# Odd-channel differences by GpSimd before the stacking transfers, with new queue orders

## The chip, the cores and the metric

The kernel runs on one core of a Trainium2 chip. The metric is the device time of one execution in microseconds (us). A core has five engines with a queue each: TensorE (PE, with its weight loads shown apart as PEld), VectorE (DVE), ScalarE (ACT), GpSimd (POOL) and SyncE (SP, which here only issues transfers). Each works through its own list in order and waits on semaphores where a value comes from another engine or from a transfer.

## The reference

The computation is a causal convolution with 15 taps and dilation 2 over 2 sequences of 16000 steps and 144 channels, to 288 channels, then a gate and a projection:

```
B, T, D, K = 2, 16000, 144, 15          # all bf16
xp = jnp.pad(x, ((0, 0), (pad, 0), (0, 0)))          # pad = (K-1)*2
h = sum over i of einsum('btc,cd->btd', xp[:, pad-2*i : pad-2*i+T, :], w[i])
f, g = h[..., :D], h[..., D:]
z = tanh(f) * sigmoid(g)
out = z @ w_o
```

## The kernel before

The 32000 time steps are cut into 128 runs of 250, one on each partition. A tile is one step of all runs; eight tiles are an oct, 31 octs follow two odd tiles at the start, and two octs (o0 = 2m+1, o1 = 2m+2) make the pair m. For each pair there are two units u (r = 0 and 1), 30 in all, each giving four tiles of either oct. The convolution is done with fewer products than 15 a tile: sums of weights meet tiles, and single weights meet differences of tiles. Tiles of x must have channels on the partitions, so they are transposed.

**The 144 channels are split.** The first 128 (DA) go through STA (a packed copy of part of Xr, the raw chunk of 16 tiles) and a DMA transpose into XA (`load_xa`). DVE then makes their differences: V, DU, DD (`v_first`, `v_second`, `v_third`) and, over octs, GX, GU, GV, GD (`g_diffs`). The last 16 channels (DB, the "odd" ones) can't fill an array, so eight taps are stacked on the partitions: XB of an oct holds in partitions 16j to 16j+15 the odd channels of the tile that lies 4j tiles back. `compact_chunk` copies them packed into C16; `load_xb(o)` transposes 128 columns of it (T16, a DMA transpose), drains T16 to a DRAM tensor s16, and fills XB's slot: partitions 32 to 127 from partitions 0 to 95 of the oct before (XB<-XB), 0 to 15 and 16 to 31 from s16 (XB<-s). `b_diffs` (DVE, line 887 by way of `tt`) then makes BD, the differences of XB's tiles, in eight tiles per oct.

**One unit on PE.** CV and CD build the terms common to both octs, which ACT copies between banks of PSUM (line 1132) and evicts to UD and UC (lines 629, 632); XC and XR build others (XS and, by DVE at line 1159, UE, which lies in Xp's room); POOL adds UC and XS into UX (`UP`, line 1169). EF adds UE and UX into the banks on DVE (line 1233, PS<-PS,Xp and PS<-PS,UX). DD closes each bank with products of GD by single weights and one product of BD by WB[v]; XR uses XB itself with WB[2] = WB[0] + WB[1]. ACT does sigmoid and tanh (`halves`), DVE multiplies them (`gate`, line 1006) into Z, a DMA transpose gives ZT, and PE projects it (line 1089) into OS, which is stored.

**Start.** The first ten outputs are computed directly with all taps (`direct`, `direct_b`, then `quad`), while weights land; XB for octs -1 and 0 comes from PE transposes evicted by ACT (line 813). DVE makes the sums of weights in that time (line 822). POOL zeroes WOR and Z and issues the 16 loads of w_o (line 1369).

**Order.** Every operation is added to a graph with what it reads and writes; `schedule` orders the five queues by a list scheduler, and `replay` changes that order by a long table of moves (MOVES) and moves some packed copies from DVE to ACT (ON_ACT, `free_copy`). Waits follow from reads, writes and buffers. `lock=True` marks DVE and POOL operations that the order keeps from overlapping. The rings: 2 chunks of Xr and C16, 2 tiles T16, 6 octs of XB, 4 octs of BD.

Of the kernel before, what the change touches and what calls it, by code (L numbers as in the profile page):

```python
# [122 lines left out]
class _Graph:  # L123
# [42 lines left out]
    def schedule(self, passes=10):  # L166

        users = {}
        for op in self.ops:
            for d in op.deps | op.soft:  # L170
                users.setdefault(d, []).append(op)
        best = None
        late, hint = {}, {}
        for _ in range(passes):
            span = self.run(users, late, hint)
            if best is None or span < best[0] - 1e-6:
                best = (span, dict((e, list(o)) for e, o in self.order.items()), [(op.start, op.end, op.bdeps, [b.phys for b in op.banks]) for op in self.ops])
            hint = dict((op, op.start) for op in self.ops)
            late = {}
            seq = {}  # L180
            extra = {}
            for a, b in zip(self.order["pe"], self.order["pe"][1:]):
                seq[a] = b
            for op in self.ops:
                for d in op.bdeps:
                    extra.setdefault(d, []).append(op)
            for op in sorted(self.ops, key=lambda o: -o.start):
# [1359 lines left out]
```

## Time and profile before

| what | value |
|---|---|
| time of one execution, median of 3 | 308.0 us (307.81 to 308.18) |
| span of the profiled execution, first to last instruction | 306.0 us |
| PE busy | 299.4 us (98%), 2553 matmuls |
| DVE busy | 288.7 us (94%) |
| ACT busy | 260.8 us (85%) |
| POOL busy | 100.1 us (33%) |
| hardware transfer queue | 47.62 MB, 67.3% of the 16 DMA engines |

The profiled execution has no time of its own beside its span; the median of the three timed ones is 2.0 us above it. Busy time is the union of an engine's instructions. A matmul is shown longer than the distance between two of them, because they are pipelined, so a busy PE can still hide gaps of a fraction of a microsecond. A wait is put down to the last thing that ended before the engine went on.

### The profile page before, as it was taken

To read this page: it belongs to the slowest core of one execution; us is meant where nothing else is said; L and a number is where in the kernel's file an instruction comes from. 1 tells how busy PE (TensorE), PEld (TensorE's weight loads), DVE (VectorE), ACT (ScalarE), POOL (GpSimd) and SP (SyncE) were. 2 spreads that over 40 slices of the span, in tenths; PEclk is the share of its full clock that TensorE was granted. 3 is DMA by queue.
4 is the path that set the end of the run, shared out by engine and by line. 5 is a ranking of instruction groups with operands and counts; after the bars stand their busy time and mean duration, and the time that the engine had idled before them with its cause. 6 is when DMAs were issued, how large, how long until landed. Compare 5 with 4: busy or idle time off the path is not lost.

```text
span 306.0 us, 7398 instructions
## 1 busy us (share of the span) xinstructions
PE 299.4 (98%) x2553; PEld 235.5 (77%) x2553; DVE 288.7 (94%) x647; ACT 260.8 (85%) x776; POOL 100.1 (33%) x89
## 2 busy tenths in 40 slices
PE   8999899999999999999999999999999999999995
PEld 7867576877877778878777778777877887777784
DVE  1899999999999999999999999999999999999855
ACT  3678588898889988888998898899888889988885
POOL 7570341233333123333222333321333331233330
PEclk9999999999999999999999999999999999999999
DMA  7978656766657675775689697996647763692643
GB/s 211 296 143 148 143 143 136 177 168 131 214 118 195 133 163 172 177 165 120 191 201 119 193 138 207 127 225 141 169 142 175 213 135 77 184 115 19 176 108 127
DMA packets 100385, 48.47 MB, mean 158 GB/s; under 512 B 88286, under 2 KB 91166, under 8 KB 100348
## 3 DMA queue, kind: packets, MB, share of 16 engines
q1 hardware_dynamic: 99801, 47.62, 67.3%
q8 instruction: 20, 0.33, 0.5%
q0 software_dynamic: 512, 0.33, 0.5%
q14 instruction: 18, 0.14, 0.2%
q10 hardware_dynamic: 34, 0.05, 0.1%
HBM read 13.77 MB, written 10.20 MB: 78 GB/s over the span
## 4 chain that ended last, share of the span: by engine, by line
PE 88%; ACT 4%; DVE 2%; DMA 2%; SPq 2%; issue 1%; DVEq 0%; ACTq 0%
PE PS L979 78%; PE PS L1089 9%; ACT STA L847 1%; DMA WA<-in_w_dram 1%; ACT TG L629 1%; DMA XB<-XB 1%; SPq L671 1%; ACT PS L1132 1%; DVE V L887 1%; DVE WC L822 0%; ACT L629 0%; SPq L874 0%; PE PS L1049 0%; ACT XB L813 0%; DVE PS L1233 0%
## 5 line engine op out<-in xcount | busy, mean ns | idle before, releaser
L1169 POOL TENSOR_TENSOR UX<-UC,XS 128x576 f32<-128x576 f32 x60 | 84.0, 1422 | 192.5 <-ACT UC L629 134.7
L979 PE MATMUL PS<-WA,GD 128*128 128x288 bf16 x450 | 87.7, 286 | 0.8 <-DVE PS L1233 0.8
L1132 ACT ACTIVATE PS<-PS 128x288 f32<-128x288 f32 x213 | 80.5, 420 | 4.5 <-PE PS L979 4.1
L629 ACT ACTIVATE TG<-PS 128x288 bf16<-128x288 f32 x194 | 68.4, 416 | 11.9 <-PE PS L979 11.4
L979 PE MATMUL PS<-WB,BD 128*128 128x288 bf16 x240 | 67.5, 286 | 0.0
L1032 ACT ACTIVATE OS<-PS 128x432 bf16<-128x432 f32 (+1 forms) x93 | 43.0, 492 | 15.5 <-PE PS L1089 14.1
L979 PEld LDWEIGHTS PS<-WA,GD 128*128 128x128 bf16 x450 | 41.9, 98 | 14.3 <-DVE PS L1233 2.1
L1233 DVE TENSOR_TENSOR PS<-PS,Xp 128x288 f32<-128x288 f32 x120 | 49.7, 458 | 1.0 <-ACT OS L1032 0.3
L1233 DVE TENSOR_TENSOR PS<-PS,UX 128x288 f32<-128x288 f32 x120 | 49.6, 456 | 0.0
L1159 DVE TENSOR_TENSOR Xp<-PS,UD 128x576 f32<-128x576 f32 x60 | 42.9, 751 | 3.0 <-PE PS L979 2.7
L979 PE MATMUL PS<-WS,GU 128*128 128x288 bf16 x210 | 44.9, 286 | 0.0
L1089 PE MATMUL PS<-WOR,ZT 128*128 128x144 bf16 (+1 forms) x322 | 40.2, 253 | 0.4 <-ACT XS L632 0.4
L979 PE MATMUL PS<-WB,XB 128*128 128x288 bf16 x140 | 38.2, 286 | 0.0
L979 PE MATMUL PS<-WC,GV 128*128 128x288 bf16 x210 | 36.2, 286 | 0.0
L979 PE MATMUL PS<-WD,DD 128*128 128x288 bf16 x210 | 32.5, 286 | 0.1
L1089 PEld LDWEIGHTS PS<-WOR,ZT 128*128 128x128 bf16 x322 | 27.6, 98 | 6.0 <-ACT XS L632 0.7
L1006 DVE TENSOR_TENSOR Z<-TG 128x576 bf16<-128x576 bf16 (+1 forms) x63 | 27.2, 439 | 2.2 <-ACT TG L629 2.2
L979 PEld LDWEIGHTS PS<-WB,BD 128*128 128x128 bf16 x240 | 23.5, 98 | 5.7
L632 ACT ACTIVATE TG<-PS 128x144 bf16<-128x144 f32 x112 | 24.6, 298 | 0.9 <-PE PS L979 0.7
L979 PEld LDWEIGHTS PS<-WD,DD 128*128 128x128 bf16 x210 | 19.6, 98 | 6.6 <-ACT PS L1132 1.2
L979 PE MATMUL PS<-WT,DU 128*128 128x288 bf16 x120 | 24.3, 286 | 0.0
L979 PEld LDWEIGHTS PS<-WS,GU 128*128 128x128 bf16 x210 | 20.3, 98 | 5.2
(94 smaller groups left out, 471.1 us busy)
## 6 DMA issues: line engine op xcount, KB each, us to landing
Xr<-in_x_dram SPq DMA_DIRECT2D x15, 576.0 KB, 4.6
out_dram<-OS SPq DMA_DIRECT2D x30, 288.0 KB, 2.6
XB<-XB SPq DMA_DIRECT2D x30, 192.0 KB, 2.9
XB<-s SPq DMA_DIRECT2D x59, 32.0 KB, 2.5
s<-T SPq DMA_DIRECT2D x30, 32.0 KB, 2.3
WA<-in_w_dram SPq DMA_DIRECT2D x2, 288.0 KB, 4.1
ZT<-Z SPq DMA_TRANSPOSE x32, 3.1
Xp<-in_x_dram SPq DMA_DIRECT2D x2, 252.0 KB, 4.2
```

Source lines behind the costliest of these rows:

```text
L629: return e.activation(bass.AP(t[:].tensor, off + (0 if st > 0 else n), [[row, NP], [st, 2], [1, n]]), bass.AP(PS[:].tensor, lo * 512 + c0, ...
L632: ins = e.activation(bass.AP(t[:].tensor, off + i * n, [[row, NP], [1, n]]), bass.AP(PS[:].tensor, q.phys * 512 + c0, [[8 * 512, NP], [1, ...
L671: return e.dma_start(tile_ap, src)
L847: g.add("act", lambda a, h=h: a.activation(STA[:, q, 4 * h:4 * h + 4, :], Xr[:, ci % NX, i0 + 4 * h:i0 + 4 * h + 4, 0:DA], ACT.Copy), r=[( ...
L979: return lambda t: t.matmul(bank(b), lhsT=lhs(), rhs=rhs(), start=start, stop=True, skip_group_check=True)
L1006: g.add("dve", lambda v: v.tensor_tensor(dst(), TG[:, s, 1, 2 * k:2 * k + n, :], TG[:, s, 0, 2 * k:2 * k + n, :], ALU.mult), r=[("TG", s, ...
L1032: return (lambda e: e.activation(dst(), src(), ACT.Copy)) if eng == "act" else (lambda e: e.tensor_copy(dst(), src()))
L1089: return t.matmul(PS[:, c0:c0 + n * D], lhsT=ZT[:, zt, blk_, :], rhs=WOR[:, wi_:wi_ + n, :].rearrange("p a b -> p (a b)"), start=first, st ...
L1132: g.add("act", lambda e: e.activation(bank(c), bank(b), ACT.Copy), r=[("bank", b)], w=[("bank", c)], dur=0.29, prio=prio)
L1159: return v.tensor_tensor(ue(u % NU, q, 0, 2).rearrange("p (v n) -> p v n", v=2), src, UD[:, u % NUD, :, :], ALU.add)
L1169: op = g.add("pool", lambda p: p.tensor_tensor(UX[:, u % NU, h, :, :], UC[:, 0, :, :], bass.AP(XS[:].tensor, h * N2, [[2 * N2, NP], [0, 2] ...
L1233: g.add("dve", lambda e, dst=dst, src=src, ua=ua: e.tensor_tensor(bank(dst), bank(src), ua(), ALU.add), r=[("bank", src), ("UX", us, h) if ...
```

## The change

Differences of the odd channels are taken before they are stacked, on x as loaded, by POOL. A chunk is loaded with two more tiles ahead of it (18, 648 KB). C16 becomes four groups of six tiles of 16 channels: for each four steps the tiles 0 and 1 themselves (a packed copy on DVE or ACT), and four differences x(t) - x(t-2) (one POOL subtraction per chunk, 128x256). One DMA transpose of three blocks and one drain follow per chunk, where there were two of one block each. XB's slot holds two groups of six tiles (2 x 768 columns) in place of eight tiles (1024 columns), so XB<-XB moves 288 KB and XB<-s 48 KB. `b_diffs` and BD are gone: DD reads its last operand from XB, with WB[0] for v = 0 and WB[3] = -WB[1] (one ACT operation at the start) for v = 1. Oct 0's slot is made by a POOL copy and a DVE subtraction from XBh, a room in UX's second half; oct 2's slot is filled from oct 0 and from s16 in four transfers, not from oct 1.

The scheduler and its moves are gone: TABLE lists the operations of every queue in order, by their numbers, and `place` sets it. ON_ACT has 11 numbers in place of 5. The table is cut below to some stretches that the prediction speaks of.

```diff
-MOVES = {
...
-ON_ACT = (212, 272, 430, 594, 1569,)
+TABLE = {
...
+    "act": ("3 4 5 33 36 51 35 63 53 61 72 43 71 79 81 112 120 110 109 121 170 96 217 142 18 97 174 102 172 107 101 106 214 241 225 243 224 184 245 183 215 261 248 253 250 194 195 263 "
...
+    "pool": ("21 19 24 22 20 75 76 77 204 208 23 113 211 82 218 198 212 201 205 206 197 207 209 199 210 203 200 202 269 270 275 348 361 408 409 430 503 517 590 749 563 564 662 676 722 "
...
+    "sp": ("2 6 7 8 9 10 11 12 13 14 15 16 17 25 26 28 213 114 111 122 118 115 116 124 123 219 117 128 126 119 127 125 258 271 220 216 226 259 304 221 228 223 229 222 426 276 227 273 "
...
+ON_ACT = (112, 217, 429, 589, 748, 1064, 1226, 1385, 1551, 1703, 2029)
...
+    def place(self, table, on_act):
+
         for i in on_act:
             op = self.ops[i]
             op.eng, op.base, op.lock = "act", op.alt, False
+        for e, text in table.items():
+            self.order[e] = [self.ops[int(x)] for x in text.split()]
         span = self.simulate()
...
-    XCH = 16
+    XCH = 18
...
+            g.add("pool", lambda p: p.tensor_copy(XB[:, bslot(0), :, 0:2, :], XBh[:, 4:12, :].rearrange("p (a b) c -> p a b c", a=2)[:, :, 0:2, :]),
+                  r=[("XBh", 0)], w=[("XB", bslot(0), 0)], dur=0.7, lock=True)
+            g.add("dve", lambda v: v.tensor_tensor(XB[:, bslot(0), :, 2:6, :].rearrange("p a b c -> p a (b c)"), XBh[:, 4:12, :].rearrange("p (a b) c -> p a (b c)", a=2),
+                                                   XBh[:, 2:10, :].rearrange("p (a b) c -> p a (b c)", a=2), ALU.subtract),
+                  r=[("XBh", -1), ("XBh", 0)], w=[("XB", bslot(0), 1)], dur=0.6, prio=2, lock=True)
...
+            free_copy(lambda: cc[:, :, 0:2, :], lambda: xr(2, 2), [("Xr", s)], [("C16", s, 0)], 0.13, 0.27)
+            g.add("pool", lambda p: p.tensor_tensor(cc[:, :, 2:6, :], xr(2), xr(0), ALU.subtract), r=[("Xr", s)], w=[("C16", s, 1)], dur=0.6, lock=True)
+            g.add("sp", lambda e: e.dma_start_transpose(T16[:, s, :, :], C16[:, s, :, :].rearrange("p a b -> p (a b)")), r=[("C16", s, 0), ("C16", s, 1)], w=[("T16", s)], dur=1.3, dma="xb", nbytes=3 * 32768)
+            g.add("sp", lambda e: e.dma_start(bass.AP(S16, ci * 384 * 128, [[128, NP], [128 * 128, 3], [1, 128]]), T16[:, s, :, :]), r=[("T16", s)], w=[("S16", ci)], dur=0.5, dma="xb", nbytes=3 * 32768)
...
+            if o != 2:
+                xdma(lambda: flatr(32, 96, s, 0, 2), lambda: flatr(0, 96, bslot(o - 1), 0, 2), xbk(o - 1), [("XB", s, 0)], 96 * GR * 4)
+            else:
+                xdma(lambda: flatr(64, 64, s, 0, 2), lambda: flatr(0, 64, bslot(0), 0, 2), xbk(0), [("XB", s, 0, 0)], 64 * GR * 4)
+                xdma(lambda: flatr(48, DB, s, 0, 1), lambda: flatr(0, DB, bslot(0), 1, 1), xbk(0), [("XB", s, 0, 1)], DB * GR * 2)
+                xdma(lambda: rows(48, DB, s, 1, 1), lambda: s16(0, 1), [("S16", 0)], [("XB", s, 0, 2)], DB * GR * 2)
+                xdma(lambda: rows(32, DB, s, 0, 2), lambda: s16(0, 2), [("S16", 0)], [("XB", s, 0)], DB * GR * 4)
+            xdma(lambda: rows(0, DB, s, 0, 2), lambda: s16(q0, 2), [("S16", ci)], [("XB", s, 2)], DB * GR * 4)
...
-        def b_diffs(o):
-            kb = xbk(o) + xbk(o - 1)
-            ef(XB, NB, bslot, BD, NBD, dslot, "BD", o, kb, True)
...
-                ops.append((lambda v=v: BD[:, dslot(o), v, 2 - 2 * k + r, :], lambda v=v: WB[:, v, :]))
+                ops.append((lambda v=v: XB[:, bslot(o), 1 - k, 4 - 2 * v + r, :], lambda v=v: WB[:, 3 * v, :]))
...
+        g.add("act", lambda a: a.activation(WB[:, 3, :], WB[:, 1, :], ACT.Copy, scale=-1.0), r=[("WB", 1)], w=[("WB", 3)], dur=0.4, prio=2)
...
-        g.schedule(5)
-        _ms = g.replay(MOVES, ON_ACT)
+        g.place(TABLE, ON_ACT)
```

The numbers count the operations in the order in which the kernel adds them: 112, 113, 114 and 115 are chunk 0's packed copy, subtraction, transpose and drain; 217 and 218 chunk 1's copy and subtraction; 430, 590, 749 and so on the subtractions of chunks 3, 4 and 5; 170 the first copy of the quad; 96 and 97 the first sigmoid and tanh; 142 the negated weights; 23 the zeroing of Z; 197 to 212 the loads of w_o; 269 and 270, and further neighbours in POOL's list such as 563 and 564, a unit's two UP additions.

More of the change, by code (lines that the diff above doesn't have):

```diff
@@ L164, in add @@
         return op
[L166 to L187, printed above, removed]
-                t = 1e9 if not (op.eng == "pe" or op in users) else span
-                for u in users.get(op, ()):
-                    if op in u.deps:
-                        t = min(t, late[u] - self.lag(op, u))
-                for u in extra.get(op, ()):
-                    t = min(t, late[u] - self.lag(op, u))
-                if op.eng == "pe":
-                    t = min(t, late[seq[op]] - op.dur) if op in seq else min(t, op.start)
-                late[op] = t
-        self.order = best[1]
-        for op, (a, b, c, d) in zip(self.ops, best[2]):
-            op.start, op.end = a, b
-            for bk, ph in zip(op.banks, d):
-                bk.phys = ph
-        return best[0]
@@ L358, in replay @@
-    def replay(self, moves, on_act):
-        self.simulate()
+    def place(self, table, on_act):
         for i in on_act:
             op = self.ops[i]
-            self.order["dve"].remove(op)
             op.eng, op.base, op.lock = "act", op.alt, False
-            seq = self.order["act"]
-            p = 0
-            while p < len(seq) and seq[p].start < op.start:
-                p += 1
-            seq.insert(p, op)
-        for e, text in moves.items():
-            seq, nums = self.order[e], [int(x) for x in text.split()]
-            for p, q in zip(nums[::2], nums[1::2]):
-                seq.insert(q, seq.pop(p))
+        for e, text in table.items():
+            self.order[e] = [self.ops[int(x)] for x in text.split()]
@@ L574, in _conv_wavenet_kernel @@
         STA = sb("STA", [NP, NST, 8, 128], BF16)
-        C16 = sb("C16", [NP, NX, XCH * DB], BF16)
-        T16 = sb("T16", [NP, 2, 128], BF16)
+        C16 = sb("C16", [NP, NX, 4, 6 * DB], BF16)
+        T16 = sb("T16", [NP, NX, 3, 128], BF16)
         XA = sb("XA", [NP, NA, 8, 128], BF16)
@@ L812, in b_halo @@
                 i0 = oct_of(tiles[0])[1]
-                g.add("act", lambda v, o=o, i0=i0, bb=bb: v.activation(XB[:, bslot(o), i0:8, :].rearrange("p a b -> p (a b)"), PSb[:, bb * 1024 + 128 * i0:bb * 1024 + 1024], ACT.Copy),
-                      r=[("bank", HB[bb])], w=[("XB", bslot(o), i) for i in range(4)], dur=0.5 if o < 0 else 0.95)
+                g.add("act", lambda v, o=o, i0=i0, bb=bb: v.activation(XBh[:, 8 * o + i0 + 4:8 * o + 12, :].rearrange("p a b -> p (a b)"), PSb[:, bb * 1024 + 128 * i0:bb * 1024 + 1024], ACT.Copy),
+                      r=[("bank", HB[bb])], w=[("XBh", o)], dur=0.5 if o < 0 else 0.95)
+            g.add("pool", lambda p: p.tensor_copy(XB[:, bslot(0), :, 0:2, :], XBh[:, 4:12, :].rearrange("p (a b) c -> p a b c", a=2)[:, :, 0:2, :]),
[3 more added lines that the diff above has]
+                  r=[("XBh", -1), ("XBh", 0)], w=[("XB", bslot(0), 1)], dur=0.6, prio=2, lock=True)
         wak = [("WA", i) for i in range(5)]
@@ L830, in load_xchunk, with xr @@
             s = ci % NX
[L831 to L833 removed]
+            return g.add("sp", ld_x(flat(Xr[:, s, 0:c - a + 2, :]), 0, NP, E0 + a - 2, E0 + c), w=[("Xr", s)], dur=0.5, dma="xr", nbytes=NP * (c - a + 2) * D * 2, soft=(chain["sp"],) if ci < 2 else ())
+        NGR = 2 * (NOCT - 1)
+        S16 = nc.dram_tensor("s16", (NGR * 6, DB, 128), BF16).ap().tensor
         def compact_chunk(ci):
[L836 removed]
             s = ci % NX
[L838 to L839 removed]
+            def xr(t, n=4):
+                return bass.AP(Xr[:].tensor, (s * XCH + t) * D + DA, [[NX * XCH * D, NP], [4 * D, 4], [D, n], [1, DB]])
+            cc = C16[:, s, :, :].rearrange("p a (t c) -> p a t c", c=DB)
+            free_copy(lambda: cc[:, :, 0:2, :], lambda: xr(2, 2), [("Xr", s)], [("C16", s, 0)], 0.13, 0.27)
+            g.add("pool", lambda p: p.tensor_tensor(cc[:, :, 2:6, :], xr(2), xr(0), ALU.subtract), r=[("Xr", s)], w=[("C16", s, 1)], dur=0.6, lock=True)
+            g.add("sp", lambda e: e.dma_start_transpose(T16[:, s, :, :], C16[:, s, :, :].rearrange("p a b -> p (a b)")), r=[("C16", s, 0), ("C16", s, 1)], w=[("T16", s)], dur=1.3, dma="xb", nbytes=3 * 32768)
+            g.add("sp", lambda e: e.dma_start(bass.AP(S16, ci * 384 * 128, [[128, NP], [128 * 128, 3], [1, 128]]), T16[:, s, :, :]), r=[("T16", s)], w=[("S16", ci)], dur=0.5, dma="xb", nbytes=3 * 32768)
         def load_xa(o):
@@ L846, in load_xa @@
                 for h in range(2):
-                    g.add("act", lambda a, h=h: a.activation(STA[:, q, 4 * h:4 * h + 4, :], Xr[:, ci % NX, i0 + 4 * h:i0 + 4 * h + 4, 0:DA], ACT.Copy),
+                    g.add("act", lambda a, h=h: a.activation(STA[:, q, 4 * h:4 * h + 4, :], Xr[:, ci % NX, i0 + 2 + 4 * h:i0 + 6 + 4 * h, 0:DA], ACT.Copy),
                           r=[("Xr", ci % NX)], w=[("STA", q, h)], dur=0.5, prio=2)
             else:
-                free_copy(lambda: STA[:, q, :, :], lambda: Xr[:, ci % NX, i0:i0 + 8, 0:DA],
+                free_copy(lambda: STA[:, q, :, :], lambda: Xr[:, ci % NX, i0 + 2:i0 + 10, 0:DA],
                           [("Xr", ci % NX)], [("STA", q, 0), ("STA", q, 1)], 0.34, 1.0)
@@ L855, in xbk @@
         def xbk(o):
-            return [("XB", bslot(o), i) for i in range(4)]
+            return [("XB", bslot(o), i) for i in range(3 if o else 2)] + ([("XB", bslot(o), 1, 0)] if o == 1 else [("XB", bslot(o), 0, i) for i in range(3)] if o == 2 else [])
         def load_xb(o):
-            s, q, ci = bslot(o), o % 2, chunk_of(8 * o)
-            c0 = (8 * o - CH[ci][0]) * DB
-            ROW = NB * 1024
+            s, ci = bslot(o), chunk_of(8 * o)
+            GR = 6 * 128
+            ROW = NB * 2 * GR
@@ L863, in xdma @@
             def xdma(out, in_, r, w, n):
                 g.add("sp", lambda e: e.dma_start(out(), in_()), r=r, w=w, dur=0.5, dma="xb", nbytes=n)
-            def rows(p0, n, slot, i0, i1):
-                return bass.AP(XB[:].tensor, p0 * ROW + slot * 1024 + i0 * 128, [[ROW, n], [128, i1 - i0], [1, 128]])
-            def flatr(p0, n, slot, i0, i1):
-                return bass.AP(XB[:].tensor, p0 * ROW + slot * 1024 + i0 * 128, [[ROW, n], [1, (i1 - i0) * 128]])
-            def s16(t, n):
-                return bass.AP(S16, t * DB * 128, [[128, DB], [DB * 128, n], [1, 128]])
@@ L874, in load_xb, with rows @@
-            g.add("sp", lambda e: e.dma_start_transpose(T16[:, q, :], C16[:, ci % NX, c0:c0 + 128]), r=[("C16", ci % NX)], w=[("T16", q)], dur=1.3, dma="xb", nbytes=32768)
-            xdma(lambda: bass.AP(S16, 8 * o * DB * 128, [[128, NP], [1, 128]]), lambda: T16[:, q, :], [("T16", q)], [("S16", o)], 32768)
-            xdma(lambda: flatr(32, 96, s, 0, 8), lambda: flatr(0, 96, bslot(o - 1), 0, 8), xbk(o - 1), [("XB", s, 0)], 196608)
-            xdma(lambda: rows(0, DB, s, 0, 8), lambda: s16(8 * o, 8), [("S16", o)], [("XB", s, 3)], 32768)
+            def rows(p0, n, slot, g0, ng):
+                return bass.AP(XB[:].tensor, p0 * ROW + (slot * 2 + g0) * GR, [[ROW, n], [128, 6 * ng], [1, 128]])
@@ new lines, in flatr, with s16 @@
+            def flatr(p0, n, slot, g0, ng):
+                return bass.AP(XB[:].tensor, p0 * ROW + (slot * 2 + g0) * GR, [[ROW, n], [1, GR * ng]])
+            def s16(q, n):
+                return bass.AP(S16, q * 6 * DB * 128, [[128, DB], [DB * 128, 6 * n], [1, 128]])
+            q0 = 2 * (o - 1)
+            if o != 2:
[5 more added lines that the diff above has]
+                xdma(lambda: rows(32, DB, s, 0, 2), lambda: s16(0, 2), [("S16", 0)], [("XB", s, 0)], DB * GR * 4)
@@ L878, in load_xb @@
+            xdma(lambda: rows(0, DB, s, 0, 2), lambda: s16(q0, 2), [("S16", ci)], [("XB", s, 2)], DB * GR * 4)
             if o > 1:
-                xdma(lambda: rows(16, DB, s, 0, 8), lambda: s16(8 * o - 4, 8), [("S16", o - 1), ("S16", o)], [("XB", s, 1), ("XB", s, 2)], 32768)
+                xdma(lambda: rows(16, DB, s, 0, 2), lambda: s16(q0 - 1, 2), [("S16", chunk_of(8 * o - 8)), ("S16", ci)], [("XB", s, 1)], DB * GR * 4)
             else:
-                xdma(lambda: flatr(16, DB, s, 0, 4), lambda: flatr(0, DB, bslot(0), 4, 8), xbk(0), [("XB", s, 1)], 16384)
@@ L882, in load_xb @@
-                xdma(lambda: rows(16, DB, s, 4, 8), lambda: s16(8, 4), [("S16", 1)], [("XB", s, 2)], 16384)
+                xdma(lambda: flatr(16, DB, s, 0, 1), lambda: flatr(0, DB, bslot(0), 1, 1), xbk(0), [("XB", s, 1, 0)], DB * GR * 2)
+                xdma(lambda: rows(16, DB, s, 1, 1), lambda: s16(0, 1), [("S16", 0)], [("XB", s, 1)], DB * GR * 2)
         TR = 128
@@ L1239, in DD @@
             p, n = UB[u][h], UB[u][2 + h]
-            we = [("D", vslot(o - i)) for i in range(4)] + [("BD", dslot(o)), ("WB", 0)] + wak
-            wf = [("D", vslot(o - i)) for i in range(4)] + [("BD", dslot(o)), ("WB", 1)] + wak
             k = part
@@ L1280, in direct_b @@
             g.add("pe", region(b, [lambda: xb_tile(e), lambda: xb_tile(e - 2)], [lambda: WB[:, 0, :], lambda: WB[:, 1, :]]),
-                  r=[("XB", bslot(o), i) for o in (-1, 0) for i in range(4)] + [("WB", 0), ("WB", 1)], w=[("bank", b)], dur=2 * MM)
+                  r=[("XBh", -1), ("XBh", 0), ("WB", 0), ("WB", 1)], w=[("bank", b)], dur=2 * MM)
         load_xchunk(0)
```

178 lines of the change are left out of this document (7 added, 171 removed), and 111 rows, old and new, of tables (MOVES, TABLE).

## The prediction

> **What bounds the kernel now.** I read the page's busy shares first, then busy time by stage, then who TensorE (PE) waits for, then the timeline at those waits.
>
> ```profile
> PE 299.4 (98%) x2553; PEld 235.5 (77%) x2553; DVE 288.7 (94%) x647; ACT 260.8 (85%) x776; POOL 100.1 (33%) x89
> ```
> ```profile
> 6.00:28.00 22.00, 21.23 (x189) 16.79 (x190) 19.73 (x56) 16.44 (x36) 10.70 (x20) 1.00 0.89 211
> 28.00:64.00 36.00, 34.55 (x279) 25.01 (x278) 34.71 (x76) 28.68 (x82) 11.67 (x8) 1.00 0.61 141
> 64.00:280.00 216.00, 216.00 (x1832) 171.01 (x1831) 215.07 (x472) 193.18 (x595) 66.80 (x49) 1.00 0.70 159
> ```
>
> The columns are length, then busy time of PE, weight loads, DVE, ACT and POOL, then granted clock and DMA share. From 64 to 280 us PE is busy 216.00 of 216.00 us at clock 1.00, beside a DVE that is busy 215.07. PE sits idle for 0.77 us from 6 to 28 us and for 1.45 us from 28 to 64 us. Waits, longest in total first, say for whom; then the places, with the row before each:
>
> ```profile
> PE PS L746 <- DVE HEAT L677: 1.1, 1, 1.1
> PE PS L979 <- DVE PS L1233: 0.8, 2, 0.6
> PE PS L979 <- ACT PS L1132: 0.7, 1, 0.7
> PE PS L1089 <- ACT XS L632: 0.4, 1, 0.4
> ```
> ```profile
> 17.17 1.39 PE L979 MATMUL PS<-WA,XA 128*128 128x288 bf16 x10
> 19.49 0.54 PE L979 MATMUL PS<-WC,V 128*128 128x288 bf16 x3 [0.68 <-ACT PS L1132]
> 34.85 0.42 PE L1089 MATMUL PS<-WOR,ZT 128*128 128x144 bf16 x3 [0.43 <-ACT XS L632]
> 35.91 0.42 PE L979 MATMUL PS<-WA,GD 128*128 128x288 bf16 x2 [0.65 <-DVE PS L1233]
> 36.91 0.29 PE L979 MATMUL PS<-WB,BD 128*128 128x288 bf16 x1
> 37.26 0.42 PE L979 MATMUL PS<-WT,XA 128*128 128x288 bf16 x2
> 44.65 0.42 PE L979 MATMUL PS<-WA,GD 128*128 128x288 bf16 x2 [0.17 <-DVE PS L1233]
> ```
>
> One matmul shows 0.29 us, yet ten in a row take 1.39: the pitch is (1.39 - 0.29) / 9 = 0.122 us. So each idle time that is shown hides another 0.29 - 0.12 = 0.17 us. The four waits at 19.49, 34.85, 35.91 and 44.65 show 0.68 + 0.43 + 0.65 + 0.17 = 1.93 us and cost 1.93 + 4 x 0.17 = 2.6 us. At 37.26 another 0.35 - 0.12 = 0.23 us goes. That is 2.8 us in places that I can name; I allow some 0.5 for smaller ones, 3.3 us in all. The change keeps all matmuls (the last one of each DD reads XB and WB[3] in place of BD and WB[1]), so nothing can be won from 64 to 280 us; it can only be lost there. The first wait (for HEAT) and the end after the last matmul depend on first loads and last stores, which stay.
>
> **The change part by part.**
>
> *DVE gives up the BD subtractions and part of the C copies.*
>
> ```profile
> L887 DVE TENSOR_TENSOR BD<-XB 128x1024 bf16<-128x1024 bf16 x25 | 16.9, 684 | 0.0
> L887 DVE TENSOR_TENSOR BD<-XB 128x512 bf16<-128x512 bf16 x10 | 4.2, 418 | 0.0
> L887 DVE TENSOR_TENSOR BD<-XB 128x1024 bf16<-128x1024 bf16 (+1 forms) x7 | 4.2, 607 | 0.0
> ```
>
> 16.9 + 4.2 = 21.1 us leave DVE over the run, of which 4.2 us lie before 64 us (third row, the window 0 to 64). One subtraction for oct 0 comes in (0.7 us, as a 128x1024 row). Past 64 us this frees an engine beside which PE does not wait: 0. Before 64 us DVE is busy 34.71 of 36 us and releases two of the four waits, so 3.5 us less in its queue is worth something there.
>
> *The chain that the second oct's odd channels made.* The chain of waits has, ahead of the wait at 35.91:
>
> ```profile
> 30.27 2.61 DMA XB<-XB
> ...
> 33.88 0.60 DVE BD L887
> ```
>
> Oct 2 had to copy oct 1's slot after that had landed. It is now filled from the drained DRAM tensor and from oct 0, without waiting for oct 1, and BD's 0.60 is gone. I count the waits at 34.85, 35.91, 37.26 (0.60 + 0.82 + 0.23 = 1.65 us) as mostly removed: 1.2. It is not all, because the DRAM route is itself late: it starts with chunk 0's GpSimd subtraction (113), which POOL's list now puts behind two WOR issues and the Z memset.
>
> ```profile
> 3.60 2.97 POOL L728 MEMSET Z<- 128x3456 bf16 x1
> 12.36 8.55 POOL L1369 DMA_DIRECT2D WOR<-in_w_o_dram  x16 [0.29 <-DMA WA<-in_w_dram]
> ```
> ```profile
> 16.29 1.22 SPq L874 DMA_TRANSPOSE T<-C  x1
> ```
>
> The WOR issues can't begin before 12.36 (they wait for the last weights); two of them are 2 x 8.55/16 = 1.1 us, the memset 2.97, the subtraction 0.9 (below): it ends near 17.3, so the first transpose goes out 1.0 us after the 16.29 of before. Against that stand the 2.61 + 0.60 us that leave the chain. At 44.65 I count 0.2 of 0.34.
>
> *ACT's new order.* Its list now puts the first copy of the quad (number 170) ahead of the first sigmoid (96) and behind four STA copies and the copy of chunk 0's odd channels (112).
>
> ```profile
> 17.43 1.28 ACT L629 ACT_TABLE_LOAD   x1
> 18.72 0.41 ACT L629 ACTIVATE TG<-PS 128x288 bf16<-128x288 f32 x1
> 19.03 0.41 ACT L1132 ACTIVATE PS<-PS 128x288 f32<-128x288 f32 x1
> 22.79 0.43 ACT L1032 ACTIVATE C<-Xr 128x256 bf16<-128x256 bf16 x1
> ```
>
> The copy that releases PE at 19.49 loses 1.28 + 0.31 us ahead of it and gains about 0.4 of copy 112: some 1.2 us earlier, more than the 0.85 that PE lost. The sigmoid and the tanh end up to 1 us later (copy 112, then chunk 1's copy, the negated WB[3] and a dummy between them), which holds their PSUM banks longer; PE has the quad's other matmuls meanwhile. I take 0.6 of 0.85. Later six more free copies lie on ACT (11 numbers against 5), at 193.18 of 216 us: room for 0.4 to 1.0 us each, hidden.
>
> *POOL's new work: 15 subtractions of 128x256 and one copy of 128x512.* No row has either form. The nearest are:
>
> ```profile
> L1169 POOL TENSOR_TENSOR UX<-UC,XS 128x576 f32<-128x576 f32 x60 | 84.0, 1422 | 192.5 <-ACT UC L629 134.7 <-ACT UC L632 43.8 <-ACT XS L632 14.0
> L804 POOL COPY XS<-Xp 128x32 bf16<-128x32 bf16 x1 | 0.5, 541 | 0.1
> 150.91 2.77 POOL L1169 TENSOR_TENSOR UX<-UC,XS 128x576 f32<-128x576 f32 x2 [6.23 <-ACT UC L629]
> 152.74 0.82 DVE L1233 TENSOR_TENSOR PS<-PS,UX 128x288 f32<-128x288 f32 x2
> ```
>
> Between 0.54 (32 elements) and 1.42 us (576), on the line through both, 256 elements cost 0.54 + 0.88 x 224/544 = 0.90 us. I take 0.9; 15 x 0.9 = 13.5 us on an engine that idles 192.5 us before UX: hidden if it runs in the 6.2 us that POOL waits for UC. The one copy lies between the same two rows, near UX's by its size, 1.3 us; it fills oct 0's slot before the first XB<-XB and lies beside the XA transposes on SP: 0. What can be uncovered is a UX pair behind a subtraction: the first UX ends at 150.91 + 1.41 = 152.32 and DVE reads it at 152.74, 0.42 us later. A subtraction that starts late enough to hold UX by more than that shows on DVE and then on PE.
>
> *The transfers.*
>
> ```profile
> XB<-XB SPq DMA_DIRECT2D x30, 192.0 KB, 2.9
> XB<-s SPq DMA_DIRECT2D x59, 32.0 KB, 2.5
> T<-C SPq DMA_TRANSPOSE x30, 2.6
> XA<-STA SPq DMA_TRANSPOSE x30, 3.3
> Xr<-in_x_dram SPq DMA_DIRECT2D x15, 576.0 KB, 4.6
> ```
>
> XB<-XB grows to 288 KB, XB<-s to 48 KB; T<-C and the drain become 15 of three blocks instead of 30 of one; Xr grows to 648 KB. Landing: XB<-XB between 2.9 and 4.6 (Xr's, twice the bytes), I take 3.2; the transposes between 2.6 and 3.3 (eight blocks), I take 2.8. SP's list has 249 numbers; its issues of before sum to 276, so 15 transposes and 15 drains go and oct 2's extra three come. A lighter queue covers a landing that is 0.3 us longer, with prefetch: the subtractions of chunks 4 and 5 (590 and 749) stand in POOL's list before the UX pair 563 and 564. Cost on the path: 0; if the cover went, 0.3 us an oct, 30 x 0.3 = 9 us.
>
> *Sum.* 1.2 + 0.2 + 0.6 = 2.0 us from the start, 0 past 64 us. The span is 306.0 and the runs' median 308.0, so 2.0 us lie around the span; the same 2.0 off the median gives 306.0.
>
> **The rivals.**
>
> *Stalls move, none goes.* The sigmoid's banks, or the later drained rows of chunk 0, hold PE where ACT and DVE no longer do. For it: the DRAM route has one more step than before (a GpSimd subtraction, and a landing of a transpose and two transfers after it). Against it: BD and the serial copy are really gone. 308.0 +- 0.6.
>
> *Slower: the subtraction ahead of UX.* The trace shows POOL held by DVE once:
>
> ```profile
> 41.92 0.68 DVE L961 TENSOR_TENSOR GU<-DU 128x1024 bf16<-128x1024 bf16 x1
> 42.52 0.45 DVE L1006 TENSOR_TENSOR Z<-TG 128x576 bf16<-128x576 bf16 x1
> 42.05 3.55 POOL L1169 TENSOR_TENSOR UX<-UC,XS 128x576 f32<-128x576 f32 x2 [4.41 <-ACT UC L629]
> ```
>
> The UX pair that began beside DVE's SBUF operations took 3.55 us instead of 2.77, 0.78 longer, which is about until they were through. The new subtraction falls into POOL's waiting time, and that is when DVE does SBUF operations; if it gets through only when DVE turns to PSUM, it stands right ahead of UX, 0.9 - 0.42 = 0.5 us too late, each chunk. Past 64 us lie some 12 of the 15 chunks (216 of about 270 us of units): 6 us, less the 2.0 won: 312. It decides from 0.42 + 2.0/12 = 0.6 us of delay. Against it: DVE has some 1.4 us less to do each chunk (21.1/15), so it can run ahead, and POOL idles over 6 us.
>
> [...]
>
> *More than counted.* All 3.3 us go: 304.7.
>
> **How the numbers follow.** Forecast 0.55 (304.9 to 307.3 by itself: 3.1 to 0.7 us won); more than that 0.05; stalls only move 0.13; the POOL rival 0.20 and longer landings 0.07, both slower. A measurement tells 0.2% (0.6 us) from no change. Faster 0.60, same 0.13, slower 0.27. The range, 304.5 to 310.0, leaves out a little below and the worst of the slower cases, together under 2 in 10.
>
> **What would show it.** Right: PE's waits on DVE PS, ACT PS and ACT XS before 64 us fall from 1.9 us to under 0.8; DVE under 272 us busy; PE full from 64 to 280 us; POOL's subtraction near 0.9 us. Wrong: PE idle past 64 us with DVE PS<-PS,UX behind it (POOL), or DMA XB as releaser (transfers), or new waits on DMA s or XB before 40 us.

## The result and the profile after

The changed kernel takes 313.1 us (median of 5, 311.91 to 314.9) against 308.0: a ratio of 1.0169, interval 1.0144 to 1.0194. It is 1.7% slower, outside the range of the prediction. Medians here are over all executions of a kernel; the ratios leave out the few that lie over 1.5% above the fastest of the same kernel. The profiled execution took 311.91 us, the shortest of the five, with a span of 310.2, against 306.0 before: 4.2 us longer.

The page's busy shares, and busy time by stage (columns as in the prediction):

```profile
PE 299.9 (97%) x2553; PEld 234.1 (75%) x2553; DVE 279.5 (90%) x607; ACT 264.0 (85%) x786; POOL 110.4 (36%) x105
```
```profile
28.00:64.00 36.00, 32.23 (x261) 23.02 (x259) 33.43 (x69) 27.13 (x75) 10.52 (x9) 1.00 0.84 184
64.00:280.00 216.00, 214.53 (x1814) 168.08 (x1813) 203.76 (x436) 195.02 (x606) 72.98 (x59) 1.00 0.82 181
```

PE does the same 2553 matmuls. It is busy 2.32 us less from 28 to 64 us (34.55 before) and 1.47 us less from 64 to 280 us, where it was full: 3.8 of the 4.2 us. The DMA share of these two stages went from 0.61 to 0.84 and from 0.70 to 0.82. PE's waits say for whom, and the timeline where:

```profile
PE PS L811 <- DMA XB<-s: 1.8, 1, 1.8
PE PS L811 <- DVE Xp L991: 1.8, 1, 1.8
PE PS L921 <- DMA ZT<-Z: 1.1, 1, 1.1
```
```profile
24.16 0.42 PE L811 MATMUL PS<-WT,XA 128*128 128x288 bf16 x2 [0.59 <-DVE WT L646]
32.66 0.28 PE L811 MATMUL PS<-WS,GU 128*128 128x288 bf16 x1 [1.83 <-DMA XB<-s]
46.59 0.42 PE L811 MATMUL PS<-WC,GX 128*128 128x288 bf16 x2 [1.83 <-DVE Xp L991]
93.43 0.54 PE L921 MATMUL PS<-WOR,ZT 128*128 128x144 bf16 x4 [1.07 <-DMA ZT<-Z]
```

The waits of before on ACT PS (19.49), ACT XS (34.85) and DVE PS (35.91, 44.65) are gone, but for 0.2 us on DVE PS. In their place stand four others. With the 0.17 us that each hides, they cost 0.8 + 2.0 + 2.0 + 1.2 = 6.0 us, against the 2.8 us named in the prediction: 3.2 of the 4.2 us. The remaining 1.0 us is not traced to a place.

**The wait at 32.66.** GpSimd's timeline (its first row as it was before, then after), then the first transpose in SP's queue, then the landing in the chain of waits:

```profile
10.37 1.09 POOL L797 MEMSET XS<- 1x512 bf16 x2 [3.81 <-ACT XS L740]
```
```profile
11.90 1.09 POOL L615 MEMSET XS<- 1x512 bf16 x2 [8.26 <-ACT XS L558]
13.06 0.60 POOL L622 COPY XS<-Xp 128x32 bf16<-128x32 bf16 x1
13.61 1.24 POOL L1200 DMA_DIRECT2D WOR<-in_w_o_dram  x2
14.85 3.00 POOL L546 MEMSET Z<- 128x3456 bf16 x1
17.79 1.08 POOL L668 TENSOR_TENSOR C<-Xr 128x256 bf16<-128x256 bf16 x1
...
20.72 6.87 POOL L1200 DMA_DIRECT2D WOR<-in_w_o_dram  x13
```
```profile
18.90 1.29 SPq L669 DMA_TRANSPOSE T<-C  x1
...
27.68 3.73 SPq L695 DMA_DIRECT2D XB<-s  x6
```
```profile
29.27 3.30 DMA XB<-s
```

The first transpose goes out at 18.90, 2.6 us later than the 16.29 of before. SP then issues with pauses of 0.1 us at most up to 31.4, so what stands behind it is late too; XB<-s lands at 29.27 + 3.30 = 32.57 and PE starts at 32.66. Before, PE came to these products at 30.77 and did not wait. Thirteen of the 16 loads of w_o now stand behind the zeroing and are issued from 20.72 to 27.6; before, all 16 were out by 20.9. They now run beside XB's transfers; the experiments below come back to this.

**The wait at 46.59.** DVE's timeline, GpSimd's and the chain:

```profile
42.43 1.90 DVE L723 TENSOR_TENSOR DD<-V 128x1024 bf16<-128x1024 bf16 x1
44.25 1.62 DVE L864 COPY STA<-Xr 128x1024 bf16<-128x1024 bf16 x1
45.79 0.74 DVE L991 TENSOR_TENSOR Xp<-PS,UD 128x576 f32<-128x576 f32 x1
```
```profile
42.32 3.26 POOL L1001 TENSOR_TENSOR UX<-UC,XS 128x576 f32<-128x576 f32 x2 [3.99 <-ACT UC L450]
```
```profile
33.79 5.31 DMA XA<-STA
```

XA<-STA took 5.31 us from its issue (median before 3.3) and released DVE late. Then GpSimd began its two UX additions just ahead of DVE's next operation. DD took 1.90 us where it takes 0.68 in the prediction's row of the same shape, and the copy 1.62 where another one, at 40.06, took 0.42: together 2.4 us, most of what PE lost. Each is 1.2 us longer, DD with two inputs and the copy with one, where one UX addition takes 1.41 us (mean of 60) and the first had begun 0.11 us before DD. That the UX pair held DVE, for one addition in each of the two, is an estimate from these lengths and starts.

This wait is not a fixed price of the change. In a second profile of the same kernel (the run for comparison below) GpSimd began 0.03 us after DD, DD ran at its usual length, only the copy was held, and PE waited 0.48 us:

```profile
41.79 3.47 POOL L1001 TENSOR_TENSOR UX<-UC,XS 128x576 f32<-128x576 f32 x2 [4.00 <-ACT UC L450]
```
```profile
41.76 0.69 DVE L723 TENSOR_TENSOR DD<-V 128x1024 bf16<-128x1024 bf16 x1
42.36 1.63 DVE L864 COPY STA<-Xr 128x1024 bf16<-128x1024 bf16 x1
```

In the fourteen profiles of this case the UX pair near this place held two DVE operations in four (PE waited 1.83 to 2.41 us), one in eight (at most 0.48) and none in two (0.17). In the four, GpSimd began before the last but one of DVE's operations ahead of Xp; in the eight, and in the kernel before, after it.

**The wait at 93.43.** SP's queue of that time, and the transfers by kind (size, median us from issue to landing):

```profile
81.58 1.05 SPq L489 DMA_DIRECT2D Xr<-in_x_dram  x1
...
86.61 2.74 SPq L904 DMA_TRANSPOSE ZT<-Z  x1
```
```profile
out_dram<-OS SPq DMA_DIRECT2D x30, 288.0 KB, 3.1
XB<-XB SPq DMA_DIRECT2D x29, 288.0 KB, 3.4
XB<-s SPq DMA_DIRECT2D x60, 48.0 KB, 3.0
ZT<-Z SPq DMA_TRANSPOSE x32, 3.5
XA<-STA SPq DMA_TRANSPOSE x30, 4.2
T<-C SPq DMA_TRANSPOSE x15, 3.2
...
q1 hardware_dynamic: 107049, 53.63, 76.5%
```

The chain has ZT<-Z from 86.61 for 6.78 us, to 93.39, where the median is 3.5; chunk 6's load of 648 KB stands ahead of it in the queue. The queue moves 53.63 MB in place of 47.62, and transfers that did not change became slower: XA<-STA from 3.3 to 4.2 us.

### The profile page after: what moved, and what is told of

Read it like the earlier page. It is cut to its first block, busy times and chain, and to the rows that moved or that the text cites. A ratio compares the mean times of both kernels' runs of the same rounds, so it can differ in the third digit from the quotient of the medians.

```text
span 310.2 us, 7389 instructions
## 1 busy us (share of the span) xinstructions
PE 299.9 (97%) x2553; PEld 234.1 (75%) x2553; DVE 279.5 (90%) x607; ACT 264.0 (85%) x786; POOL 110.4 (36%) x105
## 3 DMA queue, kind: packets, MB, share of 16 engines
q1 hardware_dynamic: 107049, 53.63, 76.5%
## 4 chain that ended last, share of the span: by engine, by line
PE 83%; DMA 8%; DVE 5%; issue 1%; SPq 1%; ACT 1%; DVEq 0%
PE PS L811 72%; PE PS L921 8%; DMA XA<-STA 4%; DMA ZT<-Z 2%; PE PS L564 1%; DMA XB<-s 1%; DVE PS L1065 1%; DVE Xp L991 1%; PE PS L592 1%; DVE V L723 1%; DVE STA L864 1%; DVE DD L723 0%; SPq L695 0%; SPq L669 0%; DVE Z L838 0%
## 5 line engine op out<-in xcount | busy, mean ns | idle before, releaser
L811 PE MATMUL PS<-WB,XB 128*128 128x288 bf16 x360 | 101.8, 286 | 0.0
L964 ACT ACTIVATE PS<-PS 128x288 f32<-128x288 f32 x213 | 81.9, 418 | 7.8 <-PE PS L811 6.4
L450 ACT ACTIVATE TG<-PS 128x288 bf16<-128x288 f32 x180 | 65.1, 418 | 6.8 <-PE PS L811 5.7
L811 PEld LDWEIGHTS PS<-WA,GD 128*128 128x128 bf16 x450 | 40.6, 98 | 15.7 <-DVE PS L1065 2.3
L811 PEld LDWEIGHTS PS<-WB,XB 128*128 128x128 bf16 x360 | 35.2, 98 | 8.7
L811 PE MATMUL PS<-WC,GV 128*128 128x288 bf16 x210 | 37.9, 286 | 0.0
L811 PE MATMUL PS<-WD,DD 128*128 128x288 bf16 x210 | 34.0, 286 | 0.0
L453 ACT ACTIVATE TG<-PS 128x144 bf16<-128x144 f32 x140 | 29.8, 301 | 2.5 <-PE PS L811 1.9
L811 PE MATMUL PS<-WC,GX 128*128 128x288 bf16 x120 | 23.5, 286 | 1.8 <-DVE Xp L991 1.8
L723 DVE TENSOR_TENSOR V<-XA 128x1024 bf16<-128x1024 bf16 (+2 forms) x38 | 23.6, 623 | 1.1 <-DMA XA<-STA 0.9
```

What stands on the lines that cost most here:

```text
L450: return e.activation(bass.AP(t[:].tensor, off + (0 if st > 0 else n), [[row, NP], [st, 2], [1, n]]), bass.AP(PS[:].tensor, lo * 512 + c0, ...
L453: ins = e.activation(bass.AP(t[:].tensor, off + i * n, [[row, NP], [1, n]]), bass.AP(PS[:].tensor, q.phys * 512 + c0, [[8 * 512, NP], [1, ...
L723: return g.add("dve", lambda v: v.tensor_tensor(dst(), a(), b(), ALU.subtract), r=r, w=wk, dur=dur, prio=2, lock=True)
L811: return lambda t: t.matmul(bank(b), lhsT=lhs(), rhs=rhs(), start=start, stop=True, skip_group_check=True)
L964: g.add("act", lambda e: e.activation(bank(c), bank(b), ACT.Copy), r=[("bank", b)], w=[("bank", c)], dur=0.29, prio=prio)
```

## The experiments

Two theories stood first: the start order (chunk 0's subtraction behind the zeroing of Z) and the larger transfers. The rival was GpSimd's new work. Each run's ratio is to the kernel before, measured beside it.

**Chunk 0's subtraction ahead of the zeroing of Z**, all else as changed; the gates wait for the zeroing.

```diff
-"21 19 24 22 20 75 76 77 204 208 23 113 211 82 218
+"21 19 24 22 20 75 76 77 204 208 113 23 211 82 218
```

> The changed kernel with one swap in POOL's list: chunk 0's subtraction goes ahead of the zeroing of Z (the gates now wait for that zeroing by name). Start-order theory: the first T<-C goes out near 16.3 us in place of 18.9, the 2.0 us that PE lost at 32.7 go, and with them part of the 2.0 at 46.6, so 313.1 becomes 309 to 311. Transfer-volume theory: the early gain is given back while the transfer engines are full, 312 to 313.5. POOL theory (subtractions hold UX or DVE all along): within 0.7 of 313.1.

311.19 us, 1.0097 (1.0069 to 1.0125). The first transpose went out at 16.85 and the wait for XB<-s shrank, but that for ZT<-Z grew:

```profile
PE PS L922 <- DMA ZT<-Z: 1.9, 1, 1.9
...
PE PS L811 <- DMA XB<-s: 0.6, 1, 0.6
```

The wait is shorter mainly because PE came 0.96 us later. The transpose was 2.05 us earlier and the XB<-s that PE needs was issued at 27.34 in place of 29.27, but it landed at 32.34 in place of 32.57:

```profile
27.34 5.01 DMA XB<-s
```

PE began these products at 32.39, against 32.66 and, in the second profile of the changed kernel, 32.12. So the place of the subtraction alone does not explain this wait.

**The sizes of before**: a chunk's load without its two extra tiles, and XB's transfers with 8 of 12 blocks from oct 3 on. XB is zeroed once by DVE at the start.

```diff
+            d = 2 if ci > 1 else 0
...
+                xdma(lambda: cut(flatr(32, 96, s, 0, 2), 8 if o > 2 else 12), lambda: cut(flatr(0, 96, bslot(o - 1), 0, 2), 8 if o > 2 else 12), xbk(o - 1), [("XB", s, 0)], 96 * GR * 4)
```

> The changed kernel with its larger transfers cut to the bytes of before: XB<-XB 192 KB and XB<-s 32 KB from oct 3 on, Xr 576 KB from chunk 2 on (so four of the twelve stacked tiles are left as they were, and two tiles of a chunk; the result of those products is not the reference's). XB is zeroed once at the start. Transfer-volume theory: landings return to before's and PE's losses at 46.6 and 93.4 shrink, 309.5 to 311. Start-order theory: the loss at 32.7 comes before any cut transfer, and what follows hangs on it, so 312 to 313.5. POOL theory: no change.

The kernel leaves a third of XB's new columns and two tiles of a chunk as they were. 310.27 us, 1.0084 (1.0054 to 1.0114), with 49.01 MB. The wait for ZT<-Z is gone, its transpose lands in 3.8 us with the smaller load still ahead of it; the early one, which has the same order behind it and the extra zeroing ahead, is longer, and PE's clock over the 5 us from 34 on was 0.66:

```profile
34.98 0.28 PE L817 MATMUL PS<-WS,GU 128*128 128x288 bf16 x1 [3.35 <-DMA XB<-s]
...
36.31 0.69 PE L817 MATMUL PS<-WS,GU 128*128 128x288 bf16 x2
```
```profile
34.00:39.00 5.00, 4.02 (x20) 2.69 (x21) 1.78 (x4) 1.44 (x3) 0.99 (x1) 0.66 0.85 207
```

**The kernel before, with every XB<-XB sent twice**, the second time into a spare slot.

```diff
-            xdma(lambda: flatr(32, 96, s, 0, 8), lambda: flatr(0, 96, bslot(o - 1), 0, 8), xbk(o - 1), [("XB", s, 0)], 196608)
+            xdma(lambda: twice(flatr(32, 96, s, 0, 8), (NB - s) * 1024), lambda: twice(flatr(0, 96, bslot(o - 1), 0, 8), 0), xbk(o - 1), [("XB", s, 0)], 196608)
```

> The kernel before, with each XB<-XB sent twice in one transfer (the second copy into a spare slot), 384 KB in place of 192: 5.8 MB more, about what the change adds (6.0 MB), and no other edit. Transfer-volume theory: 310 to 313, with PE waiting for transfers before 110 us. Start-order and POOL theories: 308.0 to 308.6.

320.2 us, 1.0375 (1.0324 to 1.0426). 53.51 MB, about as many as the changed kernel moves, cost 11 to 12 us in the order of before:

```profile
PE PS L982 <- DVE PS L1236: 3.2, 4, 2.5
PE PS L982 <- DMA XB<-s: 1.7, 1, 1.7
```

So added bytes are not covered in the kernel before either. This one doubles the very transfer that XB waits for, so this is not a price for the same bytes elsewhere.

**GpSimd's subtraction cut to one element from chunk 2 on.**

```diff
+            g.add("pool", lambda p: p.tensor_tensor(cc[:, :, 2:6, :], xr(2), xr(0), ALU.subtract) if ci < 2 else p.memset(C16[:, s, 0, 6 * DB - 1:6 * DB], 0.0), r=[("Xr", s)], w=[("C16", s, 1)], dur=0.6, lock=True)
```

> The changed kernel with POOL's subtractions from chunk 2 on replaced by a memset of one element (0.1 us in place of 0.7; the differences of later chunks stay those of the first two, so the result is not the reference's). POOL theory (my rival: the subtraction ahead of UX, or against DVE's SBUF operations): 1.5 to 5 us faster than 313.1. Start-order and transfer-volume theories: within 0.7 of 313.1.

311.44 us, 1.0110 (1.0057 to 1.0164), with the waits where they were:

```profile
PE PS L811 <- DVE Xp L991: 2.1, 1, 2.1
...
PE PS L811 <- DMA XB<-s: 1.1, 1, 1.1
```

The next run, the changed kernel once more beside other experiments, is the measure for this:

> The changed kernel as it is, on the chip and beside the runs of the others: 312 to 314 by every theory; it is the measure for the rest.

312.08 us, 1.0132 (1.0094 to 1.0170). Against the first measurement of 313.1 the cut run lies 1.7 us lower, in the band that had been set for the GpSimd theory. Against this second one it lies 0.6 us lower, the two intervals overlap widely, and the waits that the theory would remove are still there. So the subtractions past chunk 1 cost nothing that these runs can tell, with a resolution of some 2 us.

The second profile of the changed kernel also shows that its waits move from execution to execution: 1.47 us for XB<-s, 0.48 for Xp, 0.83 for ZT<-Z, and 1.53 at 50.39 for XB<-XB, which the first did not have.

**Order and sizes together** (the first two edits).

> The subtraction of chunk 0 ahead of the zeroing of Z and the larger transfers cut to the bytes of before (part of the stacked tiles left as they were, as in the cut alone). If the early loss is from the start's order and the losses at 46 and 93 us from the bytes, both go: 307.0 to 309.0. If one cause is behind both, no better than the better of the two alone: 310 to 311.5.

309.46 us, 1.0044 (1.0029 to 1.0058). PE no longer waits for ZT<-Z or Xp, but still 2.3 us for XB<-s: the first transpose went out at 16.40, and XB<-s landed at 32.59 all the same.

**The first edit, and in SP's list chunk 6's load (904) behind ZT<-Z (729)**, all bytes kept.

```diff
-438 597 904 584 750 673 592 729 747
+438 597 584 750 673 592 729 904 747
```

> The swap at the start, and the load of chunk 6 (648 KB, issued at 81.6 us in the changed kernel) moved behind the ZT<-Z transpose that was issued at 86.6 and landed at 93.4. Transfer theory (that transpose lands late because the load stands ahead of it in full transfer engines): PE's 2.0 us at 92.6 become under 0.5, and the time falls by 1 to 2 us against the swap alone, to 309.0 to 310.2. If the transpose is late by itself: no change, 311.2 +- 0.6.

309.84 us, 1.0061 (1.0041 to 1.0081). The wait for ZT<-Z is gone here too: this transpose landed 3.2 us after its issue, against 7.0 with the first edit alone. It was late because a load of 648 KB stood ahead of it in the queue.

**Two more moves on top**: the weight sum WT (150) earlier on DVE, and chunk 1's transpose (219) behind the six XB<-s.

```diff
-153 164 160 166 168 150 152
+153 164 160 150 166 168 152
...
-123 219 117 128 126 119 127 125 258
+123 117 128 126 119 127 125 219 258
```

> The same, and two more moves at the start: the weight sum WT ahead of GU and GD on DVE (PE lost 0.8 to 1.1 us for it near 25), and oct 1's and 2's XB<-s ahead of chunk 1's transpose on SP (PE lost 0.8 us for them). Start-order theory: each loss goes, 307.0 to 308.8, about the kernel before. If the transfer engines set the early landings whatever the order: 309 to 310.

311.98 us, 1.0141 (1.0090 to 1.0192): slower, though the profiled execution shows fewer early waits than the one above. The six XB<-s were issued from 24.80 on, 2.9 us sooner than in the changed kernel, and still landed between 29.3 and 32.2, beside the loads of w_o and XB<-XB, so that issuing sooner brought little. Two of the four executions had a mean clock of 0.994 and 0.995 and took 313.1 and 313.8; the other two took 310.6 and 310.9 at 1.000, which is still above most of the run before it. Why stays open.

**The zeroing of Z (23) before GpSimd's two zeroings of XS and the copy behind them (75 to 77)**, so in time in which it idles, on top of the kernel with the late chunk load; then the same with WT earlier (150 as above).

```diff
-"21 19 24 22 20 75 76 77 204 208 113 23 211
+"21 19 24 22 20 23 75 76 77 204 208 113 211
```

> As with the late chunk load, but POOL zeroes Z before its start-up work, in the time in which it idles (3.6 to 11.9 us in the changed kernel), so that chunk 0's subtraction and the loads of w_o come earlier and no zeroing stands beside DVE's work at 18 us. Start-order theory: the waits for WT (1.0 us) and for XB<-s (0.5 us) shrink below half, 308.4 to 309.4 against 309.8. If they hang on the transfer engines alone: 309.8 +- 0.5.

> Z zeroed early and the late chunk load, and on DVE the weight sum WT ahead of GU and GD. If PE's wait for WT near 25 us is a loss by itself: 0.4 to 1.0 us faster than Z early alone. If what PE gains there it waits for the next thing: no difference, +- 0.4.

309.49 us, 1.0033 (1.0001 to 1.0066), and 310.29 us, 1.0069 (1.0039 to 1.0098). The wait for XB<-s is gone in both: PE begins those products at 30.76 and 31.03. SP does not issue the six XB<-s sooner than with the late load alone (from 25.92 on, against 25.49), but the loads of w_o come 3.0 us sooner. GpSimd's loads of w_o, and the landings of XB's transfers issued between about 24 and 33 us, each first with the late load alone, then with Z zeroed early:

```profile
21.32 6.86 POOL L1201 DMA_DIRECT2D WOR<-in_w_o_dram  x13
18.29 6.87 POOL L1201 DMA_DIRECT2D WOR<-in_w_o_dram  x13
```
```profile
DMA to landing us min/median/max: 4.2/5.1/5.4
DMA to landing us min/median/max: 1.8/2.9/3.7
```

So the place of the zeroing decided the wait at 32.66. That it did so by way of the loads of w_o is read from these rows; the loads were not moved alone. In the first of the two kernels one wait of size is left in the start, 2.0 us for Xp, where DVE's DD took 1.89 us and the copy 1.61 beside a UX pair again. Moving WT gained nothing. The second kernel's waits are all 0.7 us or less beside the first one for HEAT; its ten executions fall into five from 308.9 to 309.6, the profiled one among them, and five from 311.0 to 312.4. That in the second group two DVE operations were held is possible, but not shown.

**The kernel before, with the quad's first copy ahead of the first sigmoid on ACT**: the one part of the change that the prediction valued at 0.6 us, alone.

```diff
+        seq = self.order["act"]
+        seq.remove(self.quad_copy)
+        seq.insert(seq.index(self.first_tanh[0]), self.quad_copy)
```

> The kernel before with one move: the quad's first copy goes ahead of the first sigmoid on ACT, as in the changed kernel. My step for ACT's order: PE's 0.85 us at 19.5 go and the time falls by 0.4 to 0.8 us, 307.2 to 307.6. If the later sigmoid holds its banks instead: 308.0 +- 0.2, or slower.

309.62 us, 1.0032 (0.9996 to 1.0069), which does not tell it from no change. But the ten executions fall into two groups, four from 307.0 to 307.8 and six from 309.3 to 311.6. The profiled one, 309.32, is of the second. In it the wait at 19.49 went, as priced. What followed came less than a microsecond earlier than in the kernel before, and GpSimd now started ahead of DVE:

```profile
41.40 3.31 POOL L1172 TENSOR_TENSOR UX<-UC,XS 128x576 f32<-128x576 f32 x2 [4.12 <-ACT UC L632]
```
```profile
41.56 1.89 DVE L964 TENSOR_TENSOR GU<-DU 128x1024 bf16<-128x1024 bf16 x1
43.37 1.65 DVE L1009 TENSOR_TENSOR Z<-TG 128x576 bf16<-128x576 bf16 x1
```
```profile
46.25 0.42 PE L982 MATMUL PS<-WA,GD 128*128 128x288 bf16 x2 [2.41 <-DVE PS L1236]
```

In the kernel before, DVE's GU began at 41.92 and UX at 42.05, and GpSimd was held instead (3.55 us in the prediction's row, where another pair takes 2.77), which PE did not feel. Which of two starts 0.1 to 0.2 us apart comes first goes with whether PE loses 2.4 us or 0.2.

**All edits of order, and the sizes of before** (the early zeroing, the late load, the sizes).

> Z zeroed early, the late chunk load, and the larger transfers cut to the bytes of before (part of the stacked tiles left as they were). If start order and bytes are all that makes the changed kernel slow, DVE's relief should show now: 306.5 to 308.2. If something else is left (POOL beside DVE at the start, ACT): 308.5 to 309.5.

307.31 us, 0.9974 (0.9945 to 1.0002), span 305.5:

```profile
64.00:280.00 216.00, 215.90 (x1829) 169.46 (x1827) 205.50 (x439) 196.62 (x609) 73.12 (x58) 1.00 0.73 161
```

PE is full again past 64 us, at a DMA share of 0.73. It is the only kernel whose median is below that of before, but it leaves out part of XB, as the other two with the sizes of before do, and its interval does not exclude no change.

## Why the prediction was wrong

**What held.** The wait at 19.49 went with ACT's order, as the kernel before with that one move shows. Those at 34.85 and 35.91 are gone too, also with Z zeroed early, where no wait at 32 us hides them; which part of the change did it was not tried alone. The one at 44.65 stayed, as 0.36 to 0.48 us, in five of the eight kernels where the UX pair held one DVE operation. PE did not wait for the banks of ACT's sigmoid, one of the two places that the rival of moving stalls named; the other, chunk 0's late drained rows, is part of the wait at 32.66, but the sum went well past that rival's 308. The prediction's own sign of being wrong, new waits on XB before 40 us, came.

**The step that failed: "The transfers", with "Cost on the path: 0".** It let "a lighter queue" cover the landings. The queue had fewer issues, but 6.0 MB more; the step sized the changed transfers (XB<-XB 3.2 us, measured 3.4; transposes 2.8, measured 3.2 for T<-C) and left out the unchanged ones, which go through the same queue (76.5% of the 16 engines, against 67.3%). XA<-STA went from 3.3 to 4.2 us, ZT<-Z from 3.1 to 3.5 and the stores of 288 KB from 2.6 to 3.1. At one place ZT<-Z took 6.78 us and PE lost 1.2; with the sizes of before it took 3.8, with the load behind it 3.2, and the wait was gone. The prediction's price "if the cover went" spread the loss evenly over 30 octs; it fell in a few places instead.

**The term that was mis-sized: the start's chain, 1.2 us won.** The first transpose was to come 1.0 us late and came 2.6 late. The estimate added two loads, the memset and the subtraction from 12.36 on, the time of before. But the XS zeroing and copy ahead of the loads wait for ACT, whose new order ends its XS copies later: GpSimd's zeroing begins at 11.90 in place of 10.37 and the loads at 13.61, not 12.36 (1.25 us of the 1.6 missed). The first subtraction took 1.08 us, not 0.9. The estimate then set 1.0 us against the 2.61 + 0.60 us that left another chain, as if the two cancelled, and gave no price to the 13 loads of w_o that the zeroing holds back. PE lost 2.0 us at 32.66. With the first transpose early again but the loads of w_o still late, XB<-s landed at 32.2 to 32.6; with both early the wait was gone.

**A term that was missing: GpSimd's UX pair holding DVE.** The prediction weighed that DVE holds GpSimd (3.55 us for a UX pair in place of 2.77). Ahead of 46.59 the UX pair held DVE's DD and copy for 2.4 us. That this can cost PE 2 us without any new work on GpSimd, the profile of the kernel before with one ACT copy moved shows (2.41 us at 46.25).

**The rivals.** The subtraction ahead of UX (0.20) did not come: it took 0.66 to 1.08 us, mean 710 ns, DVE waited 0.3 us for UX in the whole run, and cutting it to one element left the waits in place. The longer landings, given 0.07, came nearest. The trace of before has no row of a wait on a transfer past 64 us; that shows that the landings were covered, but not by how much.

```profile
L668 POOL TENSOR_TENSOR C<-Xr 128x256 bf16<-128x256 bf16 x15 | 10.6, 710 | 5.0 <-DMA Xr<-in_x_dram 5.0
L1065 DVE TENSOR_TENSOR PS<-PS,UX 128x288 f32<-128x288 f32 x120 | 50.1, 459 | 0.7 <-POOL UX L1001 0.3
```

**DVE's relief.** DVE is busy 279.5 us, not under 272. Of the 20.4 us that BD's removal was to bring, 9.2 show. The DD group went from 22.6 to 24.4 us and the STA copies from 10.7 (26 of them) to 11.3 (23), part of it in the two operations at 42.43 and 44.25. Most of the rest is a matter of counting: summed one by one (count times mean of its rows), DVE's instructions fell by 16 us, from 340 to 324, but busy time counts overlapping once: 51 of the 340 us overlapped, and 44 of the 324, beside more gaps (17 us before, 31 after). Past 64 us PE waited for a transfer and not for DVE, so the relief had nothing to win there, as predicted.

**How much by what.** The changed kernel measured 1.017 and 1.013. The subtraction's place alone brings it to 1.010, sizes alone to 1.008, both to 1.004, and the early zeroing, the late load and the sizes together to 0.997. What is shown: the first two edits together take back two thirds of the loss or more, and at 93 us it was the bytes and one load's place. Not shown: a price for each by itself. The interval of either edit alone overlaps that of the changed kernel's second measurement, and the waits move as soon as one is taken away.

## What to carry to other kernels

A transfer queue at 67% of its engines was not a free place to put bytes here: price the landings of the transfers that do not change (XA<-STA went from 3.3 to 4.2 us), and look for the ones that stand behind a large load (ZT<-Z landed after 7.0 us behind 648 KB, after 3.2 ahead of it). When a step at the start is moved, add up everything its queue holds ahead of it, with the waits of those steps, and look at what it pushes back: here loads were held back until they ran beside transfers that PE waited for. A gain of one microsecond at one place can shift which of two engines comes first, and that can cost more than the gain: with one ACT copy moved, PE won the 0.68 us at 19.49 and lost 2.41 at 46.25, behind a DVE operation of 1.89 us in place of 0.68. So profile the same kernel twice before a wait is taken for a property of it.

## What the runs showed that was not expected

A wait of PE sometimes cost twice here. After the 3.35 us wait above, pairs of matmuls take 0.69 us in place of 0.41 (a pitch of 0.24 us, not 0.12) until about 38.9, some 3.5 us at half pace, which is another 1.7 us. With the subtraction cut to one element, this followed a wait of 2.14 us, and the clock of the next 4 us was 0.57:

```profile
46.34 0.66 PE L811 MATMUL PS<-WC,GX 128*128 128x288 bf16 x2 [2.14 <-DVE Xp L991]
```
```profile
46.00:50.00 4.00, 3.66 (x17) 2.18 (x18) 3.44 (x9) 1.63 (x6) 0.00 (x0) 0.57 1.11 289
```

After the 1.83 us waits of the changed kernel's profile, 2.30 us with order and sizes together, and 2.41 us in the kernel before with one copy moved, it did not follow: the clock of the 4 us and more behind each is 1.00. So the length of the wait alone did not decide it: one of 2.14 us was followed by the half pace, those of 2.30 and 2.41 were not. What decides it is not shown.

The mean clock goes with much of the spread. The five executions of the changed kernel run from 311.91 us at a mean granted clock of 0.999 to 314.9 at 0.989; 0.010 x 313 = 3.1 us, against the 3.0 measured. It is not all of it: in the second measurement one execution took 312.71 us at 1.000 and another 311.02. Only one execution of each measurement was profiled, so at which wait the others lost their clock is not known. The kernel before stays at 0.998 or above in every execution.
